# The last expert's logit is taken out of the weighted sums: 136 columns instead of 137

## The chip, the cores and the metric

The kernel runs on one core of a Trainium2 chip. The core has a matrix engine (TensorE, PE in the profile, with its weight loads shown apart as PEld), a vector engine (VectorE, DVE), a scalar engine (ScalarE, ACT), a general engine (GpSimd, POOL) and a queue engine (SyncE, SP) that issues most DMA transfers. Matrix results land in PSUM, eight banks of 512 float32 values per partition; everything else is held in SBUF, 128 partitions wide. The metric is the device time of one execution in microseconds.

## What is computed

Two stages follow one another. The first is attention with a pooled key/value map; the second sends each resulting token through two of eight small adapters.

```
kv_pool = kv.reshape(B, H//4, 4, W//4, 4, C).mean(axis=(2, 4))     # B=4, C=128
kv_flat = kv_pool.reshape(B, -1, C) @ w_sr                         # 768 keys = values per batch
a = softmax(q @ kv_flat.T / sqrt(C));  x = a @ kv_flat             # 4 x 12288 tokens
logits = x @ w_gate                                                # 8 experts
topk = the two largest;  w = softmax over these two
out = x + sum over the two of  w_k * (x @ A[e]) @ B[e]             # rank 16
```

Only the difference between logits matters to the second stage: which two are the largest, and the softmax over those two.

## The kernel before

The 49152 tokens are worked through in 96 chunks of 512. A main loop over `c` (lines 653 to 718) issues, for each step, pieces of several chunks at once, so that every engine has work: the scores of chunk `c+1` or so, the weighted sums of chunk `c-1`, the turning of chunk `c-2`, and the adapters of a chunk 6 to 9 steps back (`lag`, lines 641 to 645). The order on each engine is the order in which the program writes the instructions; nothing reorders them. Waits between engines come from which tile an instruction reads or overwrites.

For one chunk:

- **Scores** (`scores`, L303 and L304): six matmuls of 512 columns, keys against queries, in three pairs; ACT takes the exponential of each pair (1024 columns) and writes it as float16 into `tt`. Two PSUM tiles (`sg`) alternate.
- **Weighted sums** (`weigh`, L315): for each of six key blocks and four groups of 128 tokens, the exponentials are the weights and `vext` streams through. A row of `vext` holds the 128 values of a key, its eight logits (the values times the gate weights, prepared in `wext`, lines 146 to 154, because the sum of logits is the logit of the sum), and a 1.0, whose sum is the softmax's denominator: 128 + 8 + 1 = `VW` = 137 columns. That makes 24 matmuls per chunk, in two halves of 12 with other PE work between. All 24 add into one PSUM tile `xps` of two banks, of which there is one, so the first half of the next chunk waits until DVE has read it.
- **Normalising** (`normalise`, L322, L326, L333): DVE takes the reciprocal of the last column, multiplies all 4 x 137 columns by it into `xn`, and finds the sorted eight logits of each token with four MAX8 instructions.
- **Gate** (`gate`, L342 to L346, once per pair of chunks): POOL works out, from the logits and the two largest, the argument of a tanh, which ACT evaluates.
- **Adapters**: PE turns the upper halves of `xn` (L382), multiplies them by A (L417), DVE applies the gates (L420), PE multiplies by B (L463), DVE adds `xn` (L477), and SP stores two chunks at a time.

`xn` is made for two chunks at once and lies in a pool `xpool` of five such tiles; its last column per token is the denominator times its reciprocal, which nothing reads. Keys and values of the next batch are prepared along the way (`values`, L197 and L199, `keys`), with sums of squares (`squares`, `ranges`) that guard against ranges in which the fast path would be inexact; a slow exact path at the end (from line 886) runs only if a check fails. The first batch is prepared before the loop by `tile_keys` and `tile_values`, after DVE has pooled its loads (L173).

The last two chunks are handled after the loop by straight code (lines 785 to 879), with `tops4` in place of `normalise`.

Of the kernel before, what the change touches and what calls it, by code (L numbers as in the profile page):

```python
# [10 lines left out]
FP32 = mybir.dt.float32  # L11
# [4 lines left out]
AF = mybir.ActivationFunctionType  # L16
ALU = mybir.AluOpType
AX = mybir.AxisListType
# [3 lines left out]
def kernel(  # L22
# [10 lines left out]
    nc = tc.nc  # L33
    P = 128
    B, N, C = q.tensor.shape
    E = 8
# [3 lines left out]
    NJ = NKV // P  # L40
    NTOK = 512
    NS = NTOK // P
    VW = C + E + 1
    CPB = N // NTOK
    NCH = B * CPB
    scale = 1.0 / float(np.sqrt(C))
# [4 lines left out]
    const = ctx.enter_context(tc.tile_pool(name="const", bufs=1))  # L51
    kvpool = ctx.enter_context(tc.tile_pool(name="kvpool", bufs=4))
    keep = ctx.enter_context(tc.tile_pool(name="keep", bufs=1))
    qpool = ctx.enter_context(tc.tile_pool(name="qpool", bufs=3))
    ttpool = ctx.enter_context(tc.tile_pool(name="ttpool", bufs=4))
    xpool = ctx.enter_context(tc.tile_pool(name="xpool", bufs=5))
    run = ctx.enter_context(tc.tile_pool(name="run", bufs=3))
    small = ctx.enter_context(tc.tile_pool(name="small", bufs=3))
    ps_t = ctx.enter_context(tc.tile_pool(name="ps_t", bufs=1, space=bass.MemoryType.PSUM))
# [3 lines left out]
        name="ps_x", bufs=1, side="right", space=bass.MemoryType.PSUM))  # L63
# [5 lines left out]
    def mtile(shape, dtype=FP32, name="hd"):  # L69
        return ps_h.tile(shape, dtype, tag="hd", name=name)  # L70

    mm = nc.tensor.matmul
# [69 lines left out]
    w_sr_sb = const.tile([P, P], FP32)  # L142
# [3 lines left out]
    wext = const.tile([P, C + E], FP32)  # L146
# [6 lines left out]
    mm(wg_ps, wT, w_gate_sb, start=True, stop=True)  # L153
    nc.vector.tensor_copy(wext[:, C:C + E], wg_ps)

    gw_all = keep.tile([P, 4, E, 2 * NS], F16, name="gw_all")
    rinv_all = keep.tile([P, NCH, NS], FP32, name="rinv_all")
    vss = keep.tile([P, 2 * B], FP32, name="vss")
    kpT, kfT, vext, sqsum = {}, {}, {}, {}
    kp_keep = keep.tile([P, B, NKV], FP32, name="kp_keep")  # L160
    for b in range(B):
        kpT[b] = kp_keep[:, b]
        if b >= 2:
            kfT[b], vext[b] = kfT[b - 2], vext[b - 2]
            continue
        kfT[b] = keep.tile([P, NKV], F16, name=f"kfT{b}")
        vext[b] = keep.tile([P, NJ, 160], F16, name=f"vext{b}")
        nc.vector.memset(vext[b][:, :, C + E:VW], 1.0)


    def sum_row(b, t, d, eng):
# [8 lines left out]
    def stile(name):  # L180
        return ps_s.tile([P, 2, NTOK], FP32, tag="sg", name=name)
# [9 lines left out]
        nc.scalar.activation(kpT[b][:, 2 * t * P:2 * (t + 1) * P], kp_ps, AF.Copy)  # L191

    def values(b, t):
        v_ps = stile("v_ps")[:, 0, 0:2 * (C + E)].rearrange("p (g e) -> p g e", g=2)
        for g in range(2):
            j = 2 * t + g
            mm(v_ps[:, g], kpT[b][:, j * P:(j + 1) * P], wext, start=(g == 0), stop=(g == 1),  # L197
               skip_group_check=True)
        nc.scalar.activation(vext[b][:, 2 * t:2 * t + 2, 0:C + E], v_ps, AF.Copy)  # L199

    def keys(b, t):

# [20 lines left out]
        nc.scalar.activation(kfT[0][:, k], k_ps, AF.Copy)  # L223

    def tile_values(t):
        v_ps = mtile([P, 2, C + E], name="v_ps")
        for g in range(2):
            j = 2 * t + g
            mm(v_ps[:, g], kpT[0][:, j * P:(j + 1) * P], wext, start=(g == 0), stop=(g == 1),
               skip_group_check=True)  # L230
        if t < NT - 1:
            nc.scalar.activation(vext[0][:, 2 * t:2 * t + 2, 0:C + E], v_ps, AF.Copy)
        else:
            nc.vector.tensor_copy(vext[0][:, 2 * t:2 * t + 2, 0:C + E], v_ps)

    def squares(b, t):

        v = vext[b][:, 2 * t:2 * t + 2, 0:C + E]
        sq = keep.tile([P, 2, C + E], FP32, name=f"sq{b}") if t == 0 else small.tile(
            [P, 2, C + E], FP32, tag="sq", name="sq", bufs=1)  # L240
        nc.gpsimd.tensor_tensor(sq, v, v, op=ALU.mult)
        if t == 0:
            sqsum[b] = sq
        else:
            nc.gpsimd.tensor_tensor(sqsum[b], sqsum[b], sq, op=ALU.add)

    def ranges(b):
        nc.vector.tensor_reduce(vss[:, b:b + 1], sqsum[b][:, :, 0:C], axis=AX.XY, op=ALU.add)
        nc.vector.tensor_reduce(vss[:, B + b:B + b + 1], sqsum[b][:, :, C:C + E], axis=AX.XY,
                                op=ALU.add)  # L250


# [37 lines left out]

    tt, xps, xpair, xn, gw, gin, xT, hg, hgT, hps = {}, {}, {}, {}, {}, {}, {}, {}, {}, {}
    garg = {}
    GRP = GROWS // NTOK

    def scores(c, r):
# [10 lines left out]
    def weigh(c, h, banks=None):  # L306
# [5 lines left out]
        for j in range(h * NH, (h + 1) * NH):  # L312
            for s in range(NS):
                o = xps[c][:, s // 2, (s % 2) * VW:(s % 2 + 1) * VW]
                mm(o, tt[c][:, j, s * P:(s + 1) * P], vext[b][:, j, 0:VW],  # L315
                   start=(j == 0 and s % 2 == 0), stop=(j == NJ - 1 and s % 2 == 1),
                   skip_group_check=True)

    def normalise(c):
        ri = rinv_all[:, c]  # L320
        xv = xps[c][:, :, 0:2 * VW].rearrange("p b (s v) -> p b s v", v=VW)
        nc.vector.reciprocal(ri.rearrange("p (b s) -> p b s", b=2), xv[:, :, :, VW - 1])  # L322
        if c % 2 == 0:
            xpair[c // 2] = xpool.tile([P, 2 * NS, VW], FP32, tag="xn", name="xn")
        xn[c] = xpair[c // 2][:, (c % 2) * NS:(c % 2 + 1) * NS]
        nc.vector.tensor_tensor(  # L326
            xn[c].rearrange("p (b s) v -> p b s v", b=2), xv,
            ri.rearrange("p (b s) -> p b s", b=2).unsqueeze(3).broadcast_to([P, 2, 2, VW]),
            op=ALU.mult)
        if c % 2 == 0:  # L330
            gin[c // 2] = small.tile([P, 2 * NS, 8], FP32, tag="top", name="top")
        for s in range(NS):
            nc.vector.max(gin[c // 2][:, (c % 2) * NS + s], xn[c][:, s, C:C + E])  # L333
# [270 lines left out]
    queries(0, 1, x_bank())  # L604
    scores(0, 0)
    tile_values(0)
    queries(0, 2, x_bank())
    scores(1, 0)
# [5 lines left out]
    warm(2)  # L614
    scores(0, 1)
    tile_values(1)
    scores(1, 1)
    weigh(0, 0)
    warm(2)
    tile_keys(2, lambda: queries(1, 0, stile("q_ps")[:, 0]))  # L620
    queries(1, 1, t_bank())
    scores(0, 2)
    tile_values(2)
    scores(2, 1)
    queries(1, 2, t_bank())
    weigh(0, 1)
    scores(1, 2)
    normalise(0)


# [7 lines left out]

    NQ = NCH // GRP

# [12 lines left out]
    for c in range(2, NCH - 1):  # L653
        b, k = divmod(c, CPB)
# [39 lines left out]
        if k in (17, 19, 21) and b + 1 < B:  # L694
            if b == 0:
                squares(0, (k - 17) // 2)
            squares(b + 1, (k - 17) // 2)
        if c in (32, 40, 56, 80):
            ranges((32, 40, 56, 80).index(c))
# [25 lines left out]
        name="ps_e", bufs=1, reuse_waits="tile", space=bass.MemoryType.PSUM))  # L725
# [57 lines left out]
    q_ = n // 2  # L783

    top = small.tile([P, 2 * NS, 8], FP32, tag="top", name="top")
    top4, top5 = top[:, 0:NS], top[:, NS:2 * NS]
    pair = xpool.tile([P, 2 * NS, VW], FP32, tag="xn", name="xn")
    xn[n - 1], xn[n] = pair[:, 0:NS], pair[:, NS:2 * NS]
    arg4, msk4, arg5, msk5 = (
        small.tile([P, NS, E], FP32, tag=f"r{i}", name=f"r{i}", bufs=1) for i in range(4))  # L790
    def tops4(c, top, y):
        ri = rinv_all[:, c]
        xv = y[:, :, 0:2 * VW].rearrange("p b (s v) -> p b s v", v=VW)
        nc.vector.reciprocal(ri.rearrange("p (b s) -> p b s", b=2), xv[:, :, :, VW - 1])
        nc.vector.tensor_tensor(
            xn[c].rearrange("p (b s) v -> p b s v", b=2), xv,
            ri.rearrange("p (b s) -> p b s", b=2).unsqueeze(3).broadcast_to([P, 2, 2, VW]),
            op=ALU.mult)
        for s in range(NS):
            nc.vector.max(top[:, s], xn[c][:, s, C:C + E])  # L800
# [6 lines left out]
    put(n - 7, add_rows(n - 7))  # L807
    weigh(n - 1, 1)
    tops4(n - 1, top4, y4)
    x_banks.close()  # L810
    ps_f = end_banks.enter_context(tc.tile_pool(
        name="ps_f", bufs=1, side="right", space=bass.MemoryType.PSUM))
# [73 lines left out]
    with tc.If(bad_v != 0):  # L886
# [4 lines left out]
        e = big2[:, 0:NKV]  # L891
# [115 lines left out]
```

## Time and profile before

| what | value |
|---|---|
| median of 3 runs | 381.48 us |
| lowest, highest | 381.07, 382.75 us |
| the profiled execution | 382.61 us |
| its span, first to last instruction | 380.8 us |
| mean granted TensorE clock | 0.995 |
| PE busy | 95% of the span |
| ACT, DVE busy | 82%, 79% |
| POOL busy | 59% |
| data moved | 100.47 MB |

The profile is of one execution. A group of instructions is named by its source line, engine, operation and tiles, followed by the count; behind the bar stand its total busy time in microseconds and the mean duration of one in nanoseconds, and then the idle time of the engine just before, with what ended it. A matmul's duration includes the time its last column needs to drain, during which the next one already streams, so the pace of matmuls is read from starts. In a timeline the first number of a row is the start in microseconds from the start of the span and the second the time that the merged group took.

### The profile page before, as it was taken

The numbers are of one execution on the slowest core, as the hardware profiler recorded it, in microseconds if no ns is written. First come the engines' busy times: TensorE is split into PE (matmuls) and PEld (weight loads), VectorE is DVE, ScalarE is ACT, GpSimd is POOL, SyncE is SP. The second block draws the span as 40 slices with busy tenths as digits, with TensorE's granted clock in tenths as the row PEclk, the third lists the DMA queues.
The fourth block names the chain that finished last, engine by engine and source line by source line (L and its number), as shares of the span: only waits on it lengthen the run. The fifth ranks groups of instructions, "written<-read, shape, count | busy, mean of one in ns | idle before, by whom it ended". The sixth has DMA issues, their size and how long they took to land.

```text
span 380.8 us, 10632 instructions
## 1 busy us (share of the span) xinstructions
PE 362.9 (95%) x3962; PEld 267.7 (70%) x3963; DVE 301.7 (79%) x951; ACT 311.1 (82%) x392; POOL 224.4 (59%) x374
## 2 busy tenths in 40 slices
PE   4989989999999999999999999999999999999993
PEld 1447757677777777777777777777777777767682
DVE  2686556878788888888888888888888898898983
ACT  1547999888888888888888988988888888888853
POOL 1002699996898877764689877755524335232244
PEclk9999999999999999999999999999999999999998
DMA  8996799999999999999999999999899799883325
GB/s 253 364 386 205 203 271 303 300 310 256 365 296 302 309 326 259 312 288 320 320 289 304 338 279 299 278 246 243 175 298 256 196 226 243 182 220 119 136 86 195
DMA packets 93465, 100.47 MB, mean 264 GB/s; under 512 B 56676, under 2 KB 56932, under 8 KB 93412
## 3 DMA queue, kind: packets, MB, share of 16 engines
q1 hardware_dynamic: 91940, 99.58, 96.1%
q8 instruction: 31, 0.51, 0.6%
q10 hardware_dynamic: 1472, 0.20, 0.3%
q14 instruction: 22, 0.18, 0.1%
HBM read 62.33 MB, written 25.90 MB: 232 GB/s over the span
## 4 chain that ended last, share of the span: by engine, by line
PE 73%; DMA 9%; DVE 7%; POOL 7%; issue 2%; ACT 1%; SPq 0%; ACTq 0%; POOLq 0%; DVEq 0%
PE xps L315 30%; PE sg L303 26%; PE d_ps L463 5%; PE t_ps L382 4%; DMA kvt<-in_kv_dram 4%; PE h_ps L417 4%; DMA b_f<-in_moe_B_dram 3%; POOL kvt L173 2%; DVE xn L326 2%; DMA ge<-g_h 2%; DVE ht L420 1%; PE v_ps L197 1%; DVE top L333 1%; POOL q L107 1%; POOL kvt L177 1%
## 5 line engine op out<-in xcount | busy, mean ns | idle before, releaser
L304 ACT ACTIVATE tt<-sg 128x1024 f16<-128x1024 f32 x288 | 277.5, 1022 | 34.8 <-PE sg L303 33.9
L303 PE MATMUL sg<-qT,kfT 128*128 128x512 f16 x576 | 170.1, 379 | 2.4 <-ACT tt L304 1.6
L315 PEld LDWEIGHTS <-tt 128*128 128x128 f16 x2304 | 148.0, 98 | 27.0 <-DVE xn L326 17.2
L315 PE MATMUL xps<-vext,tt 128*128 128x137 f16 x2256 | 166.3, 223 | 0.0
L477 DVE TENSOR_TENSOR osb<-d_ps,xn 128x512 f32<-128x512 f32 x85 | 58.7, 691 | 30.6 <-PE d_ps L463 30.4
L342 POOL TENSOR_TENSOR arg<-xn,top 128x64 f32<-128x64 f32 x47 | 14.8, 315 | 107.3 <-DVE top L333 91.5
L326 DVE TENSOR_TENSOR xn<-xps,rinv_all 128x548 f32<-128x548 f32 x94 | 68.5, 728 | 3.2
L303 PEld LDWEIGHTS <-kfT 128*128 128x128 f16 x576 | 49.3, 98 | 27.1 <-issue 3.9
L173 POOL TENSOR_TENSOR kvt<-kvt 128x1024 f32<-128x1024 f32 x27 | 63.8, 2362 | 0.2
L107 POOL CAST q<-q 128x1024 f16<-128x1024 f32 x44 | 45.7, 1038 | 26.6 <-DMA q<-in_q_dram 26.6
L420 DVE SCALAR_TENSOR_TENSOR ht<-ge,h_ps 128x512 bf16<-128x512 f16 x87 | 58.5, 672 | 0.6 <-DMA ge<-g_h 0.3
L463 PEld LDWEIGHTS <-ht 128*128 128x128 bf16 x368 | 27.2, 97 | 23.6 <-DVE ht L420 3.9
L333 DVE MAX8 top<-xn 128x8 f32<-128x8 f32 x376 | 35.1, 156 | 6.3
L393 DVE COPY xt<-t_ps 128x512 bf16<-128x512 bf16 x92 | 36.7, 399 | 0.0
L382 PE MATMUL t_ps<-id_bf,xn 128*128 128x128 bf16 x376 | 36.3, 219 | 0.0
L463 PE MATMUL d_ps<-b_bf,ht 128*128 128x128 bf16 x340 | 32.9, 219 | 0.3 <-DVE ht L420 0.2
L417 PE MATMUL h_ps<-xt,a_bf 128*128 128x512 bf16 x86 | 32.6, 379 | 0.1
L322 DVE RECIPROCAL rinv_all<-xps 128x4 f32<-128x4 f32 x94 | 17.1, 182 | 15.4 <-PE xps L315 13.1
L382 PEld LDWEIGHTS <-xn 128*128 128x128 bf16 x376 | 26.0, 98 | 0.3
L345 POOL TENSOR_SCALAR msk<-msk 128x64 f32<-128x64 f32 x47 | 20.2, 429 | 4.1
L346 POOL TENSOR_TENSOR arg<-arg,msk 128x64 f32<-128x64 f32 x47 | 15.1, 321 | 3.9
L344 POOL TENSOR_TENSOR arg<-arg,msk 128x64 f32<-128x64 f32 x47 | 15.0, 320 | 3.7
(149 smaller groups left out, 229.4 us busy)
## 6 DMA issues: line engine op xcount, KB each, us to landing
kvt<-in_kv_dram SPq DMA_DIRECT2D x48, 512.0 KB
q<-in_q_dram SPq DMA_DIRECT2D x44, 512.0 KB
out_dram<-osb SPq DMA_DIRECT2D x44, 512.0 KB
ge<-g_h SPq DMA_DIRECT2D x45, 256.0 KB
q<-in_q_dram SPq DMA_DIRECT2D x2, 1024.0 KB
out_dram<-osb SPq DMA_DIRECT2D x8, 256.0 KB
g_h<-g_sb SPq DMA_DIRECT2D x45, 16.0 KB
qT<-q SPq DMA_TRANSPOSE x44
```

The source lines that it names most:

```text
L107: nc.gpsimd.tensor_copy(q16[i], q32[i].rearrange("p k n -> p (k n)"))
L173: eng.tensor_tensor(v[:, 0], v[:, 0], v[:, d], op=ALU.add)
L303: mm(sg[:, k], kfT[b][:, j * P:(j + 1) * P], qc, start=True, stop=True)
L304: nc.scalar.activation(tt[c][:, 2 * r:2 * r + 2], sg, AF.Exp, bias=0.0, scale=scale)
L315: mm(o, tt[c][:, j, s * P:(s + 1) * P], vext[b][:, j, 0:VW], start=(j == 0 and s % 2 == 0), stop=(j == NJ - 1 and s % 2 == 1), skip_group_ ...
L326: nc.vector.tensor_tensor(xn[c].rearrange("p (b s) v -> p b s v", b=2), xv, ri.rearrange("p (b s) -> p b s", b=2).unsqueeze(3).broadcast_t ...
L333: nc.vector.max(gin[c // 2][:, (c % 2) * NS + s], xn[c][:, s, C:C + E])
L382: mm(columns(t_ps, c, s), src[:, s], id_bf, is_transpose=True, start=(s == 0), stop=(s == NS - 1), skip_group_check=True)
L417: mm(h_ps, a_bf, xT[c], start=True, stop=True)
L420: nc.vector.scalar_tensor_tensor(hgT[c].rearrange("p (k a) t -> p k (a t)", k=2), gE[c // 2][:, h:h + NS // 2].rearrange("p a t k -> p k ( ...
L463: mm(dps[c][:, s], columns(hgT[c], c, s), b_bf, start=(s == 0 and fresh), stop=(s == NS - 1), skip_group_check=True)
L477: nc.vector.tensor_tensor(osb[:, lo:hi], d, xn[c][:, lo:hi, 0:C], op=ALU.add)
```

## The change

The gate weights are reduced by the last expert's column: each of the other seven logits becomes its difference from the last one, and the last one's own is zero by construction. `vext` then holds 128 values, 7 logits and a 1.0: `VW` is 136. The streamed operand of L315 has 136 columns. The prepared matrix for the values is a new tile `wv`, filled by two DVE instructions from `wext`; `wext` itself remains for the slow path.

The eighth logit is needed by MAX8 and the gate as a value in `xn`. The five pair tiles of `xpool` become five slots of one tile `xn_all`, whose last column POOL sets to zero once, before the loop; the multiply writes only the first 135 columns of each token's row, so the zero stays. `C + E` and `VW` are both 136, so the zero takes the place where the normalised denominator would have been written. The rows of `xn` in each group of four tokens are no longer written as one run.

```diff
+    G = E - 1
-    VW = C + E + 1
+    VW = C + G + 1
...
-    xpool = ctx.enter_context(tc.tile_pool(name="xpool", bufs=5))
...
+    wv = const.tile([P, C + G], FP32)
+    nc.vector.tensor_copy(wv[:, 0:C], w_sr_sb)
+    nc.vector.tensor_scalar(wv[:, C:C + G], wext[:, C:C + G], wext[:, C + G:C + E], None,
+                            op0=ALU.subtract)
...
-        nc.vector.memset(vext[b][:, :, C + E:VW], 1.0)
+        nc.vector.memset(vext[b][:, :, C + G:VW], 1.0)
...
-            mm(v_ps[:, g], kpT[b][:, j * P:(j + 1) * P], wext, start=(g == 0), stop=(g == 1),
+            mm(v_ps[:, g], kpT[b][:, j * P:(j + 1) * P], wv, start=(g == 0), stop=(g == 1),
                skip_group_check=True)
-        nc.scalar.activation(vext[b][:, 2 * t:2 * t + 2, 0:C + E], v_ps, AF.Copy)
+        nc.scalar.activation(vext[b][:, 2 * t:2 * t + 2, 0:C + G], v_ps, AF.Copy)
...
+    xn_all = keep.tile([P, 5, 2 * NS, VW], FP32, name="xn_all")
+    nc.gpsimd.memset(xn_all[:, :, :, C + G:VW], 0.0)
...
         if c % 2 == 0:
-            xpair[c // 2] = xpool.tile([P, 2 * NS, VW], FP32, tag="xn", name="xn")
+            xpair[c // 2] = xn_all[:, c // 2 % 5]
         xn[c] = xpair[c // 2][:, (c % 2) * NS:(c % 2 + 1) * NS]
         nc.vector.tensor_tensor(
-            xn[c].rearrange("p (b s) v -> p b s v", b=2), xv,
-            ri.rearrange("p (b s) -> p b s", b=2).unsqueeze(3).broadcast_to([P, 2, 2, VW]),
+            xn[c][:, :, 0:C + G].rearrange("p (b s) v -> p b s v", b=2), xv[:, :, :, 0:C + G],
+            ri.rearrange("p (b s) -> p b s", b=2).unsqueeze(3).broadcast_to([P, 2, 2, C + G]),
             op=ALU.mult)
```

The same replacements of `C + E` by `C + G` are made in `tile_values`, `squares`, `ranges` and `tops4`. Source lines behind the change shift by 6 to 8.

More of the change, by code (lines that the diff above doesn't have):

```diff
@@ L193, in values @@
     def values(b, t):
-        v_ps = stile("v_ps")[:, 0, 0:2 * (C + E)].rearrange("p (g e) -> p g e", g=2)
+        v_ps = stile("v_ps")[:, 0, 0:2 * (C + G)].rearrange("p (g e) -> p g e", g=2)
         for g in range(2):
             j = 2 * t + g
-            mm(v_ps[:, g], kpT[b][:, j * P:(j + 1) * P], wext, start=(g == 0), stop=(g == 1),
+            mm(v_ps[:, g], kpT[b][:, j * P:(j + 1) * P], wv, start=(g == 0), stop=(g == 1),
                skip_group_check=True)
-        nc.scalar.activation(vext[b][:, 2 * t:2 * t + 2, 0:C + E], v_ps, AF.Copy)
+        nc.scalar.activation(vext[b][:, 2 * t:2 * t + 2, 0:C + G], v_ps, AF.Copy)
     def keys(b, t):
@@ L225, in tile_values @@
     def tile_values(t):
-        v_ps = mtile([P, 2, C + E], name="v_ps")
+        v_ps = mtile([P, 2, C + G], name="v_ps")
         for g in range(2):
             j = 2 * t + g
-            mm(v_ps[:, g], kpT[0][:, j * P:(j + 1) * P], wext, start=(g == 0), stop=(g == 1),
+            mm(v_ps[:, g], kpT[0][:, j * P:(j + 1) * P], wv, start=(g == 0), stop=(g == 1),
                skip_group_check=True)
         if t < NT - 1:
-            nc.scalar.activation(vext[0][:, 2 * t:2 * t + 2, 0:C + E], v_ps, AF.Copy)
+            nc.scalar.activation(vext[0][:, 2 * t:2 * t + 2, 0:C + G], v_ps, AF.Copy)
         else:
-            nc.vector.tensor_copy(vext[0][:, 2 * t:2 * t + 2, 0:C + E], v_ps)
+            nc.vector.tensor_copy(vext[0][:, 2 * t:2 * t + 2, 0:C + G], v_ps)
     def squares(b, t):
-        v = vext[b][:, 2 * t:2 * t + 2, 0:C + E]
-        sq = keep.tile([P, 2, C + E], FP32, name=f"sq{b}") if t == 0 else small.tile(
-            [P, 2, C + E], FP32, tag="sq", name="sq", bufs=1)
+        v = vext[b][:, 2 * t:2 * t + 2, 0:C + G]
+        sq = keep.tile([P, 2, C + G], FP32, name=f"sq{b}") if t == 0 else small.tile(
+            [P, 2, C + G], FP32, tag="sq", name="sq", bufs=1)
         nc.gpsimd.tensor_tensor(sq, v, v, op=ALU.mult)
@@ L248, in ranges @@
         nc.vector.tensor_reduce(vss[:, b:b + 1], sqsum[b][:, :, 0:C], axis=AX.XY, op=ALU.add)
-        nc.vector.tensor_reduce(vss[:, B + b:B + b + 1], sqsum[b][:, :, C:C + E], axis=AX.XY,
+        nc.vector.tensor_reduce(vss[:, B + b:B + b + 1], sqsum[b][:, :, C:C + G], axis=AX.XY,
                                 op=ALU.add)
@@ L786 @@
     top4, top5 = top[:, 0:NS], top[:, NS:2 * NS]
-    pair = xpool.tile([P, 2 * NS, VW], FP32, tag="xn", name="xn")
+    pair = xn_all[:, q_ % 5]
     xn[n - 1], xn[n] = pair[:, 0:NS], pair[:, NS:2 * NS]
@@ L795, in tops4 @@
         nc.vector.tensor_tensor(
-            xn[c].rearrange("p (b s) v -> p b s v", b=2), xv,
-            ri.rearrange("p (b s) -> p b s", b=2).unsqueeze(3).broadcast_to([P, 2, 2, VW]),
+            xn[c][:, :, 0:C + G].rearrange("p (b s) v -> p b s v", b=2), xv[:, :, :, 0:C + G],
+            ri.rearrange("p (b s) -> p b s", b=2).unsqueeze(3).broadcast_to([P, 2, 2, C + G]),
             op=ALU.mult)
```

## The prediction

> **What bounds the kernel now.** I read the page first, then the PE rows of the timeline in the middle of the run, then the busy time of the two matmul lines in a long stretch, and last the waits.
>
> ```profile
> span 380.8 us, 10632 instructions
> PE 362.9 (95%) x3962; PEld 267.7 (70%) x3963; DVE 301.7 (79%) x951; ACT 311.1 (82%) x392; POOL 224.4 (59%) x374
> ...
> PE xps L315 30%; PE sg L303 26%; PE d_ps L463 5%; PE t_ps L382 4%; DMA kvt<-in_kv_dram 4%; PE h_ps L417 4%; DMA b_f<-in_moe_B_dram 3%; POOL kvt L173 2%; DVE xn L326 2%; DMA ge<-g_h 2%; DVE ht L420 1%; PE v_ps L197 1%; DVE top L333 1%; POOL q L107 1%; POOL kvt L177 1%
> ...
> L303 PE MATMUL sg<-qT,kfT 128*128 128x512 f16 x576 | 170.1, 379 | 2.4 <-ACT tt L304 1.6
> L315 PEld LDWEIGHTS <-tt 128*128 128x128 f16 x2304 | 148.0, 98 | 27.0 <-DVE xn L326 17.2
> L315 PE MATMUL xps<-vext,tt 128*128 128x137 f16 x2256 | 166.3, 223 | 0.0
> L477 DVE TENSOR_TENSOR osb<-d_ps,xn 128x512 f32<-128x512 f32 x85 | 58.7, 691 | 30.6 <-PE d_ps L463 30.4
> L326 DVE TENSOR_TENSOR xn<-xps,rinv_all 128x548 f32<-128x548 f32 x94 | 68.5, 728 | 3.2
> L463 PE MATMUL d_ps<-b_bf,ht 128*128 128x128 bf16 x340 | 32.9, 219 | 0.3 <-DVE ht L420 0.2
> ```
>
> The weighted sums (L315) are the largest piece of the chain that ended last, and exactly the instruction that the change narrows. A busy PE need not be at its peak, so one chunk in the timeline of PE comes next (start, duration of the group, count):
>
> ```profile
> 196.38 0.88 PE L315 MATMUL xps<-vext,tt 128*128 128x137 f16 x12
> 197.10 0.59 PE L303 MATMUL sg<-qT,kfT 128*128 128x512 f16 x2
> 197.53 0.39 PE L463 MATMUL d_ps<-b_bf,ht 128*128 128x128 bf16 x4
> 197.76 0.88 PE L315 MATMUL xps<-vext,tt 128*128 128x137 f16 x12
> 198.48 0.39 PE L382 MATMUL t_ps<-id_bf,xn 128*128 128x128 bf16 x4
> 198.70 0.59 PE L303 MATMUL sg<-qT,kfT 128*128 128x512 f16 x2
> 199.13 0.38 PE L417 MATMUL h_ps<-xt,a_bf 128*128 128x512 bf16 x1
> 199.35 0.59 PE L303 MATMUL sg<-qT,kfT 128*128 128x512 f16 x2
> 199.78 0.88 PE L315 MATMUL xps<-vext,tt 128*128 128x137 f16 x12
> ```
>
> Starts, not ends, tell the pace: a duration includes the drain, which overlaps the next matmul. From 196.38 to 199.78 a chunk takes 3.40 us. Twelve sums take 197.10 - 196.38 = 0.72 us, 60 ns each; a 512-column matmul takes 0.43/2 = 0.215; four of 128 columns take 0.23 and 0.22. Added up, 2 x 0.72 + 7 x 0.215 + 0.45 = 3.40: no gap is left. In this stretch PE issue is the bound, and a nanosecond less per sum is a nanosecond less per chunk, 24 times.
>
> How many nanoseconds one column is worth needs more digits. These two answers give the busy time of one line's instructions in the stretch 104 to 260 us (columns: stretch, its length, PE busy and count, PEld busy and count, clock, DMA share, GB/s); the first is L315, the second L463.
>
> ```profile
> 104.00:260.00 156.00, 77.70 (x1056) 68.11 (x1056) 1.00 1.13 297
> ...
> 104.00:260.00 156.00, 17.02 (x176) 13.30 (x176) 1.00 1.13 297
> ```
>
> The clock is 1.00. A block of 12 sums is busy 11 spacings and one duration of 223 ns: 77.70/88 = 0.8830, so the spacing is (883.0 - 223)/11 = 60.0 ns. For 128 columns, blocks of four: (17.02/44 = 386.8; 386.8 - 219)/3 = 55.9 ns, give or take 0.2 for the rounded 219. One column's time follows from the durations of 512 and 128 columns: (379 - 219)/384 = 0.417 ns. From 55.9, nine more columns would make 59.7 and ten make 60.1. The measured 60.0 is nearer ten: 137 columns are paced about like 138.
>
> **The change, part by part.**
>
> *136 columns in L315.* If an odd count pays for a pair, 136 drops two columns' time: 60.0 - 0.83 = 59.2 ns. If only one column goes, 59.6. I take the pair, since the measured 60.0 lies 0.1 from the pair's figure and 0.3 from the other; the other end stays for the range. The whole kernel has 2304 sums (the count of the weight loads; some matmul records are missing): 2304 x 0.83 = 1.92 us, or 2304 x 0.42 = 0.96 us. Per chunk it is 20 or 10 ns out of 3400.
>
> [...]
>
> *Does PE then meet another wait?* The next block of sums may start only when DVE has read the single pair of banks. The rows of DVE and of the weight loads at that place, and the total of that wait:
>
> ```profile
> 197.96 0.69 DVE L477 TENSOR_TENSOR osb<-d_ps,xn 128x512 f32<-128x512 f32 x1 [0.24 <-PE d_ps L463]
> 198.68 0.18 DVE L322 RECIPROCAL rinv_all<-xps 128x4 f32<-128x4 f32 x1
> 198.90 0.73 DVE L326 TENSOR_TENSOR xn<-xps,rinv_all 128x548 f32<-128x548 f32 x1
> 199.68 0.56 PEld L315 LDWEIGHTS <-tt 128*128 128x128 f16 x8 [0.23 <-DVE xn L326]
> ...
> 38.56 0.73 DVE L326 TENSOR_TENSOR xn<-xps,rinv_all 128x548 f32<-128x548 f32 x1
> 39.35 0.89 PE L315 MATMUL xps<-vext,tt 128*128 128x137 f16 x12
> ...
> PEld L315 <- DVE xn L326: 17.2, 63, 0.5
> PE sg L303 <- ACT tt L304: 1.6, 3, 0.7
> PE sg L303 <- ACT kfT L207: 0.4, 2, 0.2
> POOL q L107 <- DMA q<-in_q_dram: 26.6, 1, 26.6
> ```
>
> DVE's result is there at 199.63; PE reaches the block at 199.35 + 0.43 = 199.78 by its own work. Where DVE ends last (38.56 + 0.73 = 39.29) the block starts 0.06 later. So 0.15 - 0.06 = 0.09 us of slack per chunk. The work that PE does meanwhile has no narrowed matmul in it, so the slack doesn't shrink with faster sums. The reciprocal at 198.68 follows the add (end 198.65) as closely as the last sum; should DVE hold it there, half of the 20 ns moves into the slack, which covers it.
>
> *The normalising multiply (L326)* handles 4 x 135 instead of 548 elements. 728 ns for 548 and 691 for 512 make 1.03 ns per element: 8 ns less. In the middle it is hidden; it counts where the sums wait for it, as at 39.35: about 9 chunks early and 8 late, 17 x 8 = 0.14 us.
>
> *Its output is no longer one run* but four runs of 135 in rows of 136. The nearest rows:
>
> ```profile
> L234 DVE CAST vext<-v_ps 128x272 f16<-128x272 f32 x1 | 0.4, 442 | 0.4 <-PE v_ps L229 0.4
> L598 DVE CAST a_bf<-a_f 128x128 bf16<-128x128 f32 x1 | 0.5, 450 | 0.0
> L601 DVE CAST b_bf<-b_half 128x128 bf16<-128x128 f32 x1 | 0.2, 228 | 0.0
> ```
>
> L234 writes two runs of 136 into rows of 160 and takes 442, against 691 - 240 x 1.03 = 444 by the slope: nothing for the break. L598 scatters 8 x 16 elements singly and takes 222 more than the flat L601. I take nothing, by the nearer row; 0.22 us is the far end.
>
> *New setup work.* DVE gets a 128 x 128 copy (0.23 by the row below) and a 7-column subtraction (at most 0.17, as the 8-column copy); POOL a memset of 40 columns.
>
> ```profile
> 2.98 0.23 DVE L147 COPY wext<-w_sr_sb 128x128 f32<-128x128 f32 x1
> 6.08 0.17 DVE L154 COPY wext<-wg_ps 128x8 f32<-128x8 f32 x1 [2.21 <-PE wg_ps L153]
> 6.21 0.09 DVE L168 MEMSET vext<- 128x6 f16 x2
> 6.84 1.22 DVE L173 TENSOR_TENSOR kvt<-kvt 128x1024 f32<-128x1024 f32 x1 [0.54 <-DMA kvt<-in_kv_dram]
> ```
>
> 0.40 us goes into the 0.54 that DVE waits for the first load: nothing. Without that cover it would cost 0.4 once. POOL's next work waits 26.6 us for its load, so the memset is free. The narrower evacuations, squares and value matmuls change two columns of work that runs some dozen times: nothing.
>
> *The ring of five pair tiles becomes one tile of five slots.* The order on every engine stays as it was, and the waits too but for two on the memset, so no late release comes in.
>
> *What is lost again.* Where PE waits for ACT (the five places above, 2.0 us) it arrives earlier and waits longer; each swallows the gain of a chunk or two: 5 x 1.5 x 20 ns = 0.15 us.
>
> Sum: 1.92 + 0.14 - 0.15 = 1.91 us. The profiled execution took 382.61 (span 380.8 and 1.8 around it), 0.3% over the median of 381.48. 382.61 - 1.91 = 380.70, a ratio of 0.9950; on the median 379.6 us.
>
> **Rivals.**
>
> *One column only.* Sums at 59.6 ns: 0.96 us less, a ratio of 0.9975, 380.5 us. For it: the pair rests on 0.3 ns between two worked-out spacings. Against it: 60.0 is the mean of 1056 matmuls.
>
> *Hidden anyway.* Something else sets the chunk: the DMA queue (share 1.13 in the stretch above), or the weights (98 ns each). Then 381.5. Against the first, POOL waited once for a query load, at the start. Against the second, loads of 98 ns are issued every 60 and every 56 ns, and the spacing moves with the columns. [...]
>
> *Slower: the broken output rows.* If L326 pays for them, PE waits as soon as it grows by more than 0.09 + 0.02 = 0.11 us, to over 0.84. At the far end of +0.22, each of some 80 chunks loses 0.11 and the 17 waiting ones 0.20: 8.8 + 3.4 = 12 us, 393 us. For it: no row shows four broken fp32 runs. Against it: L234.
>
> *More than the sum.* The late waits of PE for DVE fall with both the sums and the multiply, 28 instead of 20 ns, over all chunks: 96 x 28 ns = 2.7 us, 378.8. Against it: the slack of 0.09 in the middle.
>
> **How the numbers follow.** Two-column pacing 0.60, one column 0.12, hidden 0.08, more 0.09, slower 0.11. The forecast of 379.6 lies at the bound of 0.5% (1.9 us), about what a measurement of this kernel tells from no change, so its 0.60 splits; as the 0.15 lost to ACT is a high estimate, 0.35 goes to faster and 0.25 to no change. Faster: 0.35 + 0.09 = 0.44; same: 0.25 + 0.12 + 0.08 = 0.45; slower 0.11. The range runs from 378.8 to 381.6, which leaves out the slower case and little else.
>
> **What would show it.** In the profile after: L315 blocks of 12 at 0.71 us from start to start, busy (11 x 59.2 + 223) = 874 ns per block; the middle chunk at 3.38; L326 at 720; the wait of the weight load for L326 a little longer or equal. Wrong if the spacing is 59.6 or still 60.0, or if L326 is over 0.84 and PE waits for it in every chunk.

## The result, and the profile after

The changed kernel took 379.81 us (median; 379.71 to 380.33), the kernel before, beside it on the same chip, 381.43 us (381.07 to 382.75). The ratio is 0.9961, with a 95% interval of 0.9946 to 0.9975: 1.62 us less, by the interval 0.95 to 2.06. The profiled execution took 380.28, 0.47 over its median; the one of before was 1.2 over its own, so the two profiles lie 2.33 apart.

First the page of the changed kernel: span, busy times, the shares of the chain that ended last, and the groups that answer to those shown of before. L311 are the scores, L323 the weighted sums, L334 the multiply.

```profile
span 378.4 us, 10638 instructions
...
PE 360.1 (95%) x3963; PEld 265.8 (70%) x3963; DVE 300.9 (80%) x953; ACT 310.0 (82%) x392; POOL 224.1 (59%) x375
...
PE xps L323 28%; PE sg L311 26%; PE d_ps L471 5%; PE t_ps L390 4%; POOL kvt L179 4%; PE h_ps L425 4%; DMA q<-in_q_dram 3%; DMA ge<-g_h 2%; DVE xn_all L334 2%; DVE osb L485 2%; DVE ht L428 1%; POOL q L107 1%; POOL kvt L183 1%; POOL osb L480 1%; PE v_ps L203 1%
...
L311 PE MATMUL sg<-qT,kfT 128*128 128x512 f16 x576 | 170.1, 379 | 2.6 <-ACT tt L312 1.7 <-ACT kfT L213 0.5 <-ACT qT L579 0.3
L323 PE MATMUL xps<-vext,tt 128*128 128x136 f16 x2256 | 164.5, 223 | 0.0
L323 PEld LDWEIGHTS <-tt 128*128 128x128 f16 x2304 | 146.4, 98 | 26.9 <-DVE xn_all L334 16.6 <-issue 0.2
L334 DVE TENSOR_TENSOR xn_all<-xps,rinv_all 128x540 f32<-128x540 f32 x94 | 67.7, 720 | 3.3
```

The multiply takes 720 ns, as forecast, so its broken output costs nothing. The wait of the weight loads for it went from 17.2 to 16.6 us: no new wait took the place of the old. The duration of one sum is still 223 ns; since twelve sums take only 0.71 us from start to start (below), durations overlap, and one of them does not show the pace.

A middle chunk of the changed kernel, in the timeline of DVE and PE (start, time of the merged group; the rows are cut to one chunk and its neighbours):

```profile
197.13 0.72 DVE L334 TENSOR_TENSOR xn_all<-xps,rinv_all 128x540 f32<-128x540 f32 x1
...
197.90 0.80 PEld L323 LDWEIGHTS <-tt 128*128 128x128 f16 x12 [0.22 <-DVE xn_all L334]
198.01 0.87 PE L323 MATMUL xps<-vext,tt 128*128 128x136 f16 x12
198.72 0.59 PE L311 MATMUL sg<-qT,kfT 128*128 128x512 f16 x2
...
200.50 0.72 DVE L334 TENSOR_TENSOR xn_all<-xps,rinv_all 128x540 f32<-128x540 f32 x1
```

Twelve sums take 198.72 - 198.01 = 0.71 us, and the chunk 200.50 - 197.13 = 3.37. The multiply is done at 197.85, 0.16 before the sums start; before it was 0.15.

To see where the gain lies, both kernels are cut at the starts of the multiply of the same chunks. The two rows of each that bound chunks 8 to 20, in the timelines of before (L326) and after (L334):

```profile
59.52 0.73 DVE L326 TENSOR_TENSOR xn<-xps,rinv_all 128x548 f32<-128x548 f32 x1
...
104.04 0.73 DVE L326 TENSOR_TENSOR xn<-xps,rinv_all 128x548 f32<-128x548 f32 x1
```

```profile
58.23 0.72 DVE L334 TENSOR_TENSOR xn_all<-xps,rinv_all 128x540 f32<-128x540 f32 x1
...
102.75 0.72 DVE L334 TENSOR_TENSOR xn_all<-xps,rinv_all 128x540 f32<-128x540 f32 x1
```

This stretch takes 44.52 us before and 44.52 after. All stretches, from such starts (us):

| chunks | before | after | difference | 20 ns a chunk |
|---|---|---|---|---|
| 0 to 8 | 27.21 | 27.10 | -0.11 | -0.16 |
| 8 to 20 | 44.52 | 44.52 | 0.00 | -0.24 |
| 20 to 30 | 34.98 | 34.81 | -0.17 | -0.20 |
| 30 to 45 | 53.08 | 52.81 | -0.27 | -0.30 |
| 45 to 58 | 45.47 | 45.25 | -0.22 | -0.26 |
| 58 to 75 | 60.79 | 60.53 | -0.26 | -0.34 |
| 75 to 93 | 64.52 | 64.49 | -0.03 | -0.36 |
| 93 to the end | 17.90 | 17.79 | -0.11 | |

In four stretches the gain is near the forecast step. In 8 to 20 it is gone entirely. The differences add up to 1.17 us, less than the 1.62 between the medians, though inside the interval; two profiled executions can't show where the other 0.45 lies. The first multiply started 1.18 us earlier after (31.13 against 32.31). In all profiled executions of this document it lies between 30.77 and 33.79, and the kernel that differs from before in one unused column has it at 30.77: this is the loading at the start, and none of it is counted as a gain.

The chain that ended last, of the changed kernel, shows what the stretch 8 to 20 runs through (start, time on the chain):

```profile
67.09 2.33 POOL kvt L179
69.49 1.27 POOL kvt L183
70.83 0.72 POOL kvt L184
...
73.08 0.33 POOL arg L354
73.43 0.32 ACT gw_all L366
73.75 0.28 ACT kfT L213
...
74.07 0.59 PE sg L311 x2
```

POOL adds the rows of the next batch's values and keys (`kvt`), only then ends a gate (`arg`), ACT's tanh (`gw_all`) waits for the gate, the keys (`kfT`) that ACT makes next come late, and PE's scores (`sg`) wait for them. The narrowed matmul is not what this part of the chain waits for. The same happens once more, with scores that start at 88.97 (90.17 before); behind them the chain runs through PE. Up to these scores the stretch is 0.09 us longer than before, and behind them 0.09 shorter.

### The profile page after: what moved, and what is told of

Read it like the earlier page. It is cut to its first block, busy times and chain, and to the rows that moved or that the text cites. A ratio compares the mean times of both kernels' runs of the same rounds, so it can differ in the third digit from the quotient of the medians.

```text
span 378.4 us, 10638 instructions
## 1 busy us (share of the span) xinstructions
PE 360.1 (95%) x3963; PEld 265.8 (70%) x3963; DVE 300.9 (80%) x953; ACT 310.0 (82%) x392; POOL 224.1 (59%) x375
## 4 chain that ended last, share of the span: by engine, by line
PE 71%; POOL 11%; DVE 7%; DMA 4%; issue 2%; ACT 2%; SPq 1%; POOLq 0%; DVEq 0%
PE xps L323 28%; PE sg L311 26%; PE d_ps L471 5%; PE t_ps L390 4%; POOL kvt L179 4%; PE h_ps L425 4%; DMA q<-in_q_dram 3%; DMA ge<-g_h 2%; DVE xn_all L334 2%; DVE osb L485 2%; DVE ht L428 1%; POOL q L107 1%; POOL kvt L183 1%; POOL osb L480 1%; PE v_ps L203 1%
## 5 line engine op out<-in xcount | busy, mean ns | idle before, releaser
L311 PE MATMUL sg<-qT,kfT 128*128 128x512 f16 x576 | 170.1, 379 | 2.6 <-ACT tt L312 1.7
L323 PEld LDWEIGHTS <-tt 128*128 128x128 f16 x2304 | 146.4, 98 | 26.9 <-DVE xn_all L334 16.6
L323 PE MATMUL xps<-vext,tt 128*128 128x136 f16 x2256 | 164.5, 223 | 0.0
L485 DVE TENSOR_TENSOR osb<-d_ps,xn_all 128x512 f32<-128x512 f32 x85 | 58.7, 690 | 30.8 <-PE d_ps L471 30.1
L350 POOL TENSOR_TENSOR arg<-xn_all,top 128x64 f32<-128x64 f32 x47 | 14.5, 309 | 107.3 <-DVE top L341 91.7
L334 DVE TENSOR_TENSOR xn_all<-xps,rinv_all 128x540 f32<-128x540 f32 x94 | 67.7, 720 | 3.3
L311 PEld LDWEIGHTS <-kfT 128*128 128x128 f16 x576 | 49.4, 98 | 27.4 <-issue 4.7
L341 DVE MAX8 top<-xn_all 128x8 f32<-128x8 f32 x376 | 35.2, 155 | 6.4
L390 PE MATMUL t_ps<-id_bf,xn_all 128*128 128x128 bf16 x376 | 36.3, 219 | 0.0
L390 PEld LDWEIGHTS <-xn_all 128*128 128x128 bf16 x376 | 25.9, 98 | 0.3
L354 POOL TENSOR_TENSOR arg<-arg,msk 128x64 f32<-128x64 f32 x47 | 15.0, 319 | 3.9
L366 ACT ACTIVATE gw_all<-arg 128x64 f16<-128x64 f32 x45 | 14.1, 313 | 3.9 <-POOL arg L354 3.9
```

Of the source, the lines that this page charges most:

```text
L311: mm(sg[:, k], kfT[b][:, j * P:(j + 1) * P], qc, start=True, stop=True)
L323: mm(o, tt[c][:, j, s * P:(s + 1) * P], vext[b][:, j, 0:VW], start=(j == 0 and s % 2 == 0), stop=(j == NJ - 1 and s % 2 == 1), skip_group_ ...
L334: nc.vector.tensor_tensor(xn[c][:, :, 0:C + G].rearrange("p (b s) v -> p b s v", b=2), xv[:, :, :, 0:C + G], ri.rearrange("p (b s) -> p b ...
L390: mm(columns(t_ps, c, s), src[:, s], id_bf, is_transpose=True, start=(s == 0), stop=(s == NS - 1), skip_group_check=True)
L485: nc.vector.tensor_tensor(osb[:, lo:hi], d, xn[c][:, lo:hi, 0:C], op=ALU.add)
```

## The experiments

The theory after the result: sums are paced by pairs of columns, so 2304 x 0.83 ns comes out of PE's work, and about 0.3 us of it is swallowed where POOL, not PE, sets the time. The rivals: one column only, with other gains; DVE as the second bound; a loss in the tail.

**One more column before, one and two fewer after.** `e1_138` widens the streamed operand of the kernel before by an unused column; `e2_135` and `e3_134` take one and two more logits out of the changed kernel's sums.

```diff
-    VW = C + E + 1
+    VW = C + E + 2
```

> The kernel before with a second column of ones, so that the sums have 138 columns. Theory of pairs: 137 is already paced like 138, so the spacing stays at 60.0 ns, the busy time of a block of 12 at 0.883 us, and the time is that of before within 0.1% (a ratio of 0.999 to 1.002; the multiply on DVE grows by 4 elements, 4 ns, where the sums wait for it: 0.07 us). Rival, one column 0.417 ns each: 60.4 ns, 2304 x 0.417 = 0.96 us more, a ratio of 1.0025. The GpSimd add of the last chunks (1182 ns in before, 1268 in after) gets rows of 138 instead of 137 words: if even rows make it slow, it is near 1268 here too.

```diff
-    G = E - 1
+    G = E - 2
...
-    nc.vector.tensor_scalar(wv[:, C:C + G], wext[:, C:C + G], wext[:, C + G:C + E], None,
+    nc.vector.tensor_scalar(wv[:, C:C + G], wext[:, C:C + G], wext[:, C + E - 1:C + E], None,
...
-    xn_all = keep.tile([P, 5, 2 * NS, VW], FP32, name="xn_all")
-    nc.gpsimd.memset(xn_all[:, :, :, C + G:VW], 0.0)
+    xn_all = keep.tile([P, 5, 2 * NS, C + E], FP32, name="xn_all")
+    nc.gpsimd.memset(xn_all[:, :, :, C + G:C + E], 0.0)
```

> The kernel after with one logit fewer: sums of 135 columns. It leaves out the seventh expert's logit (set to that of the eighth), so its routing is not the reference's. Theory of pairs: 135 is paced like 136, spacing 59.2 ns as in after, time as after within 0.1% (ratio to before 0.995 to 0.997). Rival, one column each: 58.8 ns, 0.96 us less than after, ratio 0.9935.

The same edit with `G = E - 3`:

> The kernel after with two logits fewer: sums of 134 columns. It leaves out the sixth and seventh experts' logits. Both theories: spacing 58.3 ns, 1.92 us less than after in the rate of the matmuls; theory of pairs puts the whole step between 135 and 134, the rival half of it. If the gain per pair reaches the end as in after (1.6 of 1.92 us), ratio to before about 0.992.

Below is the same row for each kernel: the sums' line alone in a stretch that holds 115 whole blocks of 12 (columns: stretch, its length, PE busy and count, PEld busy and count, clock, DMA share, GB/s). Before (137 columns):

```profile
54.00:258.90 204.90, 101.54 (x1380) 88.97 (x1379) 1.00 1.13 301
```

138 columns:

```profile
52.50:257.35 204.85, 101.54 (x1380) 88.98 (x1379) 1.00 1.14 301
```

After (136):

```profile
52.70:256.85 204.15, 100.45 (x1380) 88.02 (x1380) 1.00 1.12 302
```

135 columns:

```profile
52.70:256.75 204.05, 100.45 (x1380) 88.01 (x1379) 1.00 1.13 302
```

134 columns:

```profile
52.70:257.60 204.90, 99.32 (x1380) 87.04 (x1379) 1.00 1.12 301
```

101.54 twice, 100.45 twice, then 99.32. Per block that is 883.0, 873.5 and 863.7 ns; less the duration of the block's last sum (223.0, 222.6 and 222.0 ns on average) and over 11 spacings, one sum takes 60.0 ns at 138 and 137 columns, 59.2 at 136 and 135, and 58.3 at 134. The starts of the sums give the same. An odd count costs what the next even one costs, and a pair costs 0.83 ns. That is shown by the steps themselves, without the price of a column from other lines.

The steps belong to these float16 sums. The value matmuls (`v_ps`, L197 before, L203 after) work in float32 and became narrower in the same kernels: 136, 135, 134 and 133 columns start 115.9, 115.0, 114.2 and 113.3 ns apart (means of the 27 spacings in each profile that hold no other wait). There every single column counts. Why the two differ is open.

The whole times follow: 138 columns 381.62 (ratio 1.0000, 0.9973 to 1.0027), 135 columns 379.82 (0.9952, 0.9936 to 0.9967), beside 381.44 for before; 134 columns 379.08 (0.9932, 0.9907 to 0.9956). The profiled execution of 134 columns took 380.56, since it lost 1.4 us in the stretch 45 to 58 (46.68 us), where PE waits for queries (`qT`) that a transfer brings late: over its whole profile the scores (L311) wait 1.2 us for it. With 135 the stretch 75 to 93 took 64.18, 0.34 below before and 0.31 below the changed kernel. The waits in this stretch, of the changed kernel and with 135 columns (us in total, times, longest):

```profile
DVE ht L428 <- DMA ge<-g_h: 0.7, 1, 0.7
```

```profile
DVE ht L428 <- DMA ge<-g_h: 0.4, 1, 0.4
```

DVE's wait for the gates' bytes from DRAM differs by that much; in before it is 0.3. So the missing gain of this stretch in the table goes with one late transfer of the profiled execution, and with a shorter wait nearly all of the gain is there. In the profiles below of kernels with 136 columns this wait is 0.2 to 0.7 us, in those with 137 at most 0.4; whether the change makes it longer on average is not shown.

**How much slack the multiply has.** An instruction of DVE is put between the reciprocal and the multiply of every chunk of the changed kernel, first a small memset, then a copy of 128 x 128 whose result nobody reads.

```diff
+    idle = keep.tile([P, P], FP32, name="idle")
...
+        nc.vector.memset(idle[:, 0:6], 0.0)
```

> The kernel after with an idle VectorE memset of 128x6 (some 0.06 us) between the reciprocal and the normalising multiply of every chunk of the main loop. Theory of the slack (0.09 us in before, 0.10 to 0.11 in after, of which nothing is used): the middle chunk keeps its period of 3.38 us; only the chunks whose sums wait for the multiply pay, some 17 of them, together about 1 us. Rival, no slack: 3.44 us per chunk in the middle, 5 us in all.

```diff
+        nc.vector.tensor_copy(idle, w_sr_sb)
```

> The same with a VectorE copy of 128x128 float32 (0.23 us) in place of the memset. Theory of the slack: beyond it every chunk pays the rest, 0.23 - 0.11 = 0.12 us: 3.50 us per chunk in the middle, about 80 x 0.12 + 17 x 0.23 = 13.5 us in all. Rival, no slack: 3.61 us, 22 us in all. Rival, VectorE is hidden altogether: 3.38 us.

The small one says nothing on the slack: it ran within the gap that DVE leaves between reciprocal and multiply anyway. Rows of its timeline:

```profile
199.76 0.18 DVE L332 RECIPROCAL rinv_all<-xps 128x4 f32<-128x4 f32 x1
199.90 0.06 DVE L333 MEMSET idle<- 128x6 f32 x1
199.98 0.72 DVE L337 TENSOR_TENSOR xn_all<-xps,rinv_all 128x540 f32<-128x540 f32 x1
```

From the reciprocal to the multiply it is 0.22, as before (198.68 to 198.90), and a middle chunk stayed at 3.38. Its 382.8 us, of a single execution, holds a loading phase 2.7 us longer than the changed kernel's.

With the copy the kernel took 400.32 us (also a single execution), far over what was expected, because the copy was not 0.23 us long. Its row in the view of its line (shortest, median, longest):

```profile
L333 DVE COPY idle<-w_sr_sb x94: 194/393/2345, 31.3 to 380.6; 128x128 f32<-128x128 f32 x94
```

Two chunks of its timeline, one where the copy was short and one where it wasn't:

```profile
207.26 0.20 DVE L333 COPY idle<-w_sr_sb 128x128 f32<-128x128 f32 x1
207.38 0.72 DVE L337 TENSOR_TENSOR xn_all<-xps,rinv_all 128x540 f32<-128x540 f32 x1
208.26 0.87 PE L323 MATMUL xps<-vext,tt 128*128 128x136 f16 x12
...
210.49 1.04 POOL L107 CAST q<-q 128x1024 f16<-128x1024 f32 x1
210.54 0.18 DVE L332 RECIPROCAL rinv_all<-xps 128x4 f32<-128x4 f32 x1
210.64 0.97 DVE L333 COPY idle<-w_sr_sb 128x128 f32<-128x128 f32 x1
211.53 0.71 DVE L337 TENSOR_TENSOR xn_all<-xps,rinv_all 128x540 f32<-128x540 f32 x1
212.29 0.88 PE L323 MATMUL xps<-vext,tt 128*128 128x136 f16 x12 [0.49 <-DVE xn_all L337]
```

The second copy ends at 211.61, 0.08 us after POOL's cast (210.49 + 1.04 = 211.53). So does every long one: all 54 copies of more than 250 ns end 0.08 to 0.09 us after an instruction of POOL, and the longest, 2345 ns, lasted through nearly the whole of one of POOL's sums (2346). Why a copy lasts until POOL's instruction has ended is not shown. This run measures something else than it was built for, but its many delays still give the slack: over the chunks PE's stall is the multiply's delay less about 0.12 us (0.77 late gives a stall of 0.65, 0.38 late gives 0.26). The rows shown agree: undisturbed, the sums start 0.16 after the multiply's end (197.85 to 198.01), delayed, 0.05 after it (212.24 to 212.29), which leaves 0.11. The forecast had 0.09, and 8 ns more from the shorter multiply.

**The tail.** The rows of `xn_all` are 136 words apart, those of `xn` were 137. `e4_pitch137` gives the changed kernel the old distance.

```diff
-    xn_all = keep.tile([P, 5, 2 * NS, VW], FP32, name="xn_all")
+    xn_all = keep.tile([P, 5, 2 * NS, VW + 1], FP32, name="xn_all")
```

> The kernel after with rows of 137 words in xn_all, of which 136 are used; nothing else changes. Theory: the row pitch of 136 words makes the three GpSimd adds of the last chunks 86 ns longer each (1268 against 1182), and they stand in the chain that ends last: they fall back to 1182 and the time falls by up to 0.26 us against after, a ratio to before about 0.9955. Rival: the place in memory or the single tile does it: the adds stay at 1268 and the ratio at 0.996.

POOL's last adds onto the output, in the view of their line (shortest, median, longest), first before, then after, then with the old distance:

```profile
L472 POOL TENSOR_TENSOR osb<-osb,xn x3: 1182/1182/1183, 370.3 to 374.4; 128x512 f32<-128x512 f32 x3
```

```profile
L480 POOL TENSOR_TENSOR osb<-osb,xn_all x3: 1267/1268/1276, 368.0 to 372.2; 128x512 f32<-128x512 f32 x3
```

```profile
L480 POOL TENSOR_TENSOR osb<-osb,xn_all x3: 1181/1183/1183, 368.3 to 372.4; 128x512 f32<-128x512 f32 x3
```

At 136 words each add takes 86 ns more; at 137, and at 138 in `e1_138` (1182), it doesn't. DVE's adds of the same rows (L485, 690 ns on average; L477 before, 691) don't change. In the changed kernel all three of POOL's adds stand on the chain that ended last, in the other two only the last two. What it costs shows in the tail: from the multiply of chunk 93 to the end it is 17.90 before, 17.79 after, and 17.64 with the old distance, so 0.15 us. The whole time did not show it: 380.31 us (ratio 0.9967, 0.9948 to 0.9985), not below the changed kernel. An effect of 0.15 us is under what these runs tell apart.

**POOL's row sums spread out.** The stretch 8 to 20 holds groups of three row sums per tile of the next batch, at steps that two lists give. The next three runs move those steps: `e5_spread_before` in the kernel before, `e6_spread_after` the same in the changed kernel, and `e11_even_after` another way in the changed kernel.

```diff
-            sm = [5, 5, 7, 9, 9, 11, 13, 13, 15]
-            st = [10, 14, 18]
+            sm = [5, 6, 8, 9, 11, 12, 14, 16, 17]
+            st = [11, 15, 19]
```

> The kernel before, with GpSimd's row sums for the second batch spread more evenly over the main loop's steps (never two in one step, the last at step 17 instead of 15; pooling steps 11, 15, 19 instead of 10, 14, 18). Theory that GpSimd sets the pace between the multiplies of chunks 8 and 20 (44.5 us for 12 chunks in before and in after alike): this stretch gets shorter, by some 1 us, since 12 chunks at PE's pace of 3.4 us and some 2 us of preparing matmuls would take 43; total about 380.4. Rival, ACT's own work sets it: the stretch stays at 44.5 and the total at 381.4.

> The kernel after with the same spreading. Theory of GpSimd's pace: with GpSimd out of the way, the 136 columns show in this stretch as well: it is 12 x 20 ns = 0.24 us shorter than in the spread kernel before, and the distance between the two spread kernels is 1.85 us, against 1.62 without spreading. Rival, ACT's own work: both stretches stay at 44.5 us and the distance at 1.6.

```diff
-            sm = [5, 5, 7, 9, 9, 11, 13, 13, 15]
+            sm = [6, 6, 8, 8, 10, 10, 12, 14, 14]
```

> The kernel after with all of its work, the second batch's row sums issued in even steps only, that is right behind the gate and the cast of a step and not ahead of the next gate (steps 6, 6, 8, 8, 10, 10, 12, 14, 14 instead of 5, 5, 7, 9, 9, 11, 13, 13, 15). Theory that what hurts is the gate queued behind two sums: ACT's waits for the gate (3.9 us in after) shrink, the stretch falls by 0.3 to 1 us and the total to about 379.3. Rival, the amount of GpSimd's work alone counts: 44.5 us and 379.8 stay.

All three became slower: 387.04 us (1.0137, 1.0108 to 1.0166), 384.87 (1.0086, 1.0052 to 1.0120) and 384.94 (1.0101, 1.0082 to 1.0119). The stretch 8 to 20 took 49.40, 47.62 and 49.34 instead of 44.52. The waits of the first show why (us in total, times, longest):

```profile
PE sg L303 <- ACT kp_keep L191: 3.9, 2, 2.4
PE kp_ps L189 <- POOL kvt L178: 0.5, 1, 0.5
```

PE now waits for the end of the row sums themselves. My expectation took the sums for movable and left out that what reads them has its own fixed step. These runs show that the stretch hangs on where POOL's sums stand. They don't tell how much of the gain it swallowed, since the two kernels of the pair met different waits.

**Less work on POOL.** One of the three row sums per tile of the second batch is left out in both kernels, `e9_less_before` and `e10_less_after`.

```diff
-            sums.setdefault(c0 + k, []).append((b, i // 3, i % 3 + 1))
+            if b > 1 or i % 3 != 1:
+                sums.setdefault(c0 + k, []).append((b, i // 3, i % 3 + 1))
```

> The kernel before without one of GpSimd's three row sums per tile of the second batch (it leaves out a quarter of that batch's pooling, so its attention is not the reference's): 3 x 2.36 = 7.1 us of GpSimd's work fewer, all between the multiplies of chunks 4 and 18, and nothing added or moved. Theory that GpSimd's work, by way of the gates that ACT waits for, sets the pace between chunks 8 and 20: that stretch falls from 44.5 to about 43 (12 chunks at 3.4 and some 2 us of preparing matmuls), the total by 1 to 1.5 us. Rival, ACT's own work sets it: 44.5 stays.

> The kernel after with the same left out. Theory of GpSimd's pace: with it out of the way the stretch is shorter than in the kernel above by 12 x 20 ns = 0.24 us (before and after are alike in it at 44.52 and 44.53), and the two kernels are 1.85 us apart. Rival: the two are again alike in that stretch.

The starts that bound chunks 8 to 20, of the kernel before with less on POOL:

```profile
58.02 0.73 DVE L327 TENSOR_TENSOR xn<-xps,rinv_all 128x548 f32<-128x548 f32 x1
...
101.33 0.73 DVE L327 TENSOR_TENSOR xn<-xps,rinv_all 128x548 f32<-128x548 f32 x1
```

And of the changed kernel with less on POOL:

```profile
58.11 0.72 DVE L335 TENSOR_TENSOR xn_all<-xps,rinv_all 128x540 f32<-128x540 f32 x1
...
101.20 0.72 DVE L335 TENSOR_TENSOR xn_all<-xps,rinv_all 128x540 f32<-128x540 f32 x1
```

43.31 against 43.09 us: with POOL out of the way the stretch gains 0.22, near 12 chunks at 20 ns (0.24). With POOL at its full work it gained nothing. So the lost quarter of a microsecond lies there, and with fewer of POOL's sums it comes back, by one profile of each kernel. By whole times the two are 379.88 (0.9958, 0.9943 to 0.9972) and 378.76 (0.9927, 0.9912 to 0.9942), 1.12 apart instead of the 1.85 that I expected, a difference that these intervals hardly tell apart. In the profile of the second, a wait for the gates' bytes of 0.7 us, which ends at 327.7 us and which the first doesn't have, takes back what the stretch gives: chunks 75 to 93 take 64.55 against 64.27. Whether that wait stood in its other executions too is not seen.

**The tanh later.** If POOL's late gate holds ACT and with it PE, it helps to let ACT come to the tanh one step later. `e12_late_tanh` does that to the changed kernel, for pairs 1 to 9, with nothing left out.

```diff
+    late = {}
...
-        sent[2 * p + 3] = p
+        late[p] = 1 if 1 <= p <= 9 else 0
+        sent[2 * p + 3 + late[p]] = p
...
-        if c >= 3 and c % 2 == 1:
-            gate_tanhs((c - 3) // 2)
+        for p in {(c - 4) // 2, (c - 3) // 2}:
+            if p >= 0 and 2 * p + 3 + late.get(p, 0) == c:
+                gate_tanhs(p)
```

> The kernel after with all of its work; for pairs 1 to 9 the tanh of the gates, and the sending of them, is issued one step later, so that ACT no longer stands and waits for GpSimd's gate in front of its exponentials (those waits were 3.9 us in after and 1.4 us with a third of the row sums left out). GpSimd's work is unchanged. Theory that GpSimd sets the pace of the stretch between chunks 8 and 20 by way of these waits: the stretch falls from 44.5 to about 43.1, as when GpSimd's work was cut, and the total to about 378.5. Rival, GpSimd's amount of work holds the stretch by its other products as well (the casts of the queries, the pooled tiles): it stays near 44.5, and the total at 379.8 or above.

The waits between 57 and 103 us, first of the changed kernel:

```profile
ACT gw_all L366 <- POOL arg L354: 2.3, 4, 0.9
...
PE sg L311 <- ACT kfT L213: 0.5, 2, 0.3
PE sg L311 <- ACT tt L312: 0.3, 1, 0.3
```

None of these three is left with the later tanh; what is left for the weight loads is this:

```profile
PEld L323 <- DVE xn_all L334: 0.9, 4, 0.2
```

The stretch 8 to 20 takes 43.09 us with POOL's full work, as with less of it, and in it the chain that ended last runs through PE alone (shares of the chain by line, 57 to 103 us):

```profile
by line: PE xps L323 40.1%; PE sg L311 36.9%; PE t_ps L390 6.3%; PE d_ps L471 5.8%; PE h_ps L425 5.6%; PE v_ps L203 3.3%; PE kp_ps L195 1.4%; PE k_ps L211 0.7%; issue 0.1%
```

So the rival, that the amount of POOL's work holds the stretch, falls: what held it is ACT standing before POOL's late gate. The kernel before was not run with the later tanh, so a pair that differs in the columns alone is not there for this edit.

The whole took 379.39 us (ratio to before 0.9945, 0.9927 to 0.9964; single times 377.93 to 380.81). By the median it beats both kernels, but its interval overlaps the changed kernel's, and of the 1.43 us that the stretch gained in the profile the medians show 0.42. What takes the rest in the other executions isn't seen.

## Why the prediction was right, and where its sum was off

*The forecast.* 379.6 us was forecast, 379.81 measured; the ratio 0.9950 lies inside the measured interval (0.9946 to 0.9975). The likeliest case came, and the total is not told apart from the forecast. The profiles say more than the total: by them one term was mis-sized, one was missed, and one is not confirmed.

*Two columns for one: right.* 60.0 to 59.2 ns was forecast and measured, 874 ns of busy time per block forecast and 873.5 measured, 3.38 us per chunk forecast and found in the middle. 138 and 137 columns, and 136 and 135, cost the same. The rival of one column only (59.6 ns, 380.5 us) falls by that.

*The weights and the queue as bound (hidden anyway): wrong.* The spacing went down by a step at each of two pairs with a weight load of 98 ns beside every matmul.

*The broken output rows at no cost: right.* 720 ns forecast and measured, so the slower rival (393 us) had no ground. The slack that it counted on is 0.12 instead of 0.09.

*The multiply's 8 ns where the sums wait for it (0.14 us): not confirmed.* Over chunks 0 to 8 the gain is 0.11 us, 14 ns a chunk, where 28 was counted; the late stretch 58 to 75 gained 15 a chunk. In both profiles the sums start within 0.06 us of the multiply's end, and so wait for it, at 12 chunks, not at 17. No run isolates the term. The rival of more than the sum needed 28 ns over all chunks, and no stretch of the table shows it.

*Lost again at the waits (0.15 us): mis-sized.* I found the five waits of PE for ACT and let each swallow a chunk or two. The time between such waits belongs to POOL's chain as well, so the loss is counted over chunks 8 to 20 as a whole: 0.24 us of PE's work, and the rows show none of it gained. What the last chunks gained, the part ahead of them had lost. The two runs with less on POOL show 0.22 of it come back.

*The ring as five slots of one tile: the term that was missed.* I looked at its waits and order, which did hold, and not at the rows' distance, which made POOL's last adds 86 ns longer each, 0.15 us of the tail. The single run that restored the distance shortened the stretch, not measurably the whole.

*Setup at nothing: right.* The subtraction, which follows the new copy, and the first row sum of the changed kernel, in the timeline of DVE:

```profile
6.43 0.22 DVE L159 TENSOR_SCALAR wv<-wext 128x7 f32<-128x7 f32 x1
...
6.87 1.23 DVE L179 TENSOR_TENSOR kvt<-kvt 128x1024 f32<-128x1024 f32 x1 [0.16 <-DMA kvt<-in_kv_dram]
```

DVE still waits 0.16 us for the first load, instead of 0.54. The wait covered it.

Together: 1.91 less 0.09 for the wait term (0.24 instead of 0.15) and 0.15 for the adds would be 1.67, beside 1.62 measured. That closeness is luck. The interval is 1.1 us wide, and the table of stretches, which holds all that the profiled pair gained behind the first multiply, adds up to 1.17; 0.33 of what it lacks against 20 ns a chunk goes with the late transfer in 75 to 93, and with 135 columns, at the same pace, the same stretches add up to 1.53. That the two terms exist is shown in the profiles; that they make up the difference of the totals is only argued.

## What to carry to other kernels

Look for pairs in the streamed columns of a float16 matmul: in these sums an odd width paid for the next even one (60.0 ns at 138 and 137 columns, 59.2 at 136 and 135, 58.3 at 134), so taking one column from an odd width was worth two, and from an even width nothing. For another type, measure it first: this kernel's float32 matmuls paid for each column (115.9, 115.0, 114.2 and 113.3 ns at 136 to 133). Before adding a gain over all steps, cut the trace into stretches and ask for each whether the gain's engine sets its length; a stretch that another engine paces can swallow all of it, as chunks 8 to 20 did (44.52 us before and after), and not only what its visible waits suggest. A tile that is laid out anew has a new distance between rows, and each engine that reads it is to be timed again: here POOL's add went from 1182 to 1268 ns, DVE's stayed at 690 to 691.

## What the runs showed of the hardware that was not expected

- The pace of the float16 sums goes in steps of two columns: 60.0, 60.0, 59.2, 59.2 and 58.3 ns for 138, 137, 136, 135 and 134 columns. That of the float32 value matmuls goes by single columns: 115.9, 115.0, 114.2 and 113.3 ns for 136, 135, 134 and 133.
- POOL's add of 128 x 512 fp32 values took 1268 ns where one operand's rows of 128 lie 136 words apart, and 1182 to 1183 where they lie 137 or 138 apart; DVE's add of the same rows kept its 690 to 691. Why is open.
- A DVE copy of 128 x 128 fp32 values within SBUF, 0.20 us long at best, took up to 2.35 us and ended, where it was long, 0.08 to 0.09 us after the end of an instruction of POOL; the multiply beside it, which reads PSUM, took 0.71 us on average, no more than without the copy (0.72).
